# A decode-attention kernel whose TensorE program shrinks from 1307 to 449 instructions by loops over registers

## The chip, the core and the metric

The kernel runs on one core of one Trainium2 chip. A core has engines that run their own instruction streams and meet through semaphores: TensorE (PE, matrix products; loading of weights is shown as PEld), VectorE (DVE), ScalarE (ACT), GpSimd (POOL) and SyncE (SP), which here only issues DMAs. Sixteen DMA engines move data between the memory outside (DRAM) and the core's SBUF; PSUM takes the results of TensorE. The metric is the device time of one execution in microseconds (us); lower is better.

## What is computed

Two independent attention blocks, A and B, of one decode step each. `x` is one row of 512, there are 32 heads of 128, and the caches hold 8192 positions. Everything is bf16 in memory.

```python
q = (x @ wq).reshape(B, Sq, H, Dh).transpose(0, 2, 1, 3)       # 1 x 32 x 1 x 128
scores = einsum("bhqd,bhkd->bhqk", q, k_cache) * (Dh ** -0.5)  # 8192 per head
p = softmax(scores, axis=-1)
o = einsum("bhqk,bhkd->bhqd", p, v_cache)
y = o.transpose(0, 2, 1, 3).reshape(B, Sq, H * Dh) @ wo        # 512 per block
# output: concatenate([y of A, y of B], axis=-1)
```

The two pairs of caches hold 268 MB of the 285 MB that are read; each element is used once.

## The kernel before

The 64 heads form 16 groups of four (`N = 16`, groups 0 to 7 of A, 8 to 15 of B). A group is one round. Its K, 8 MiB, lies in SBUF with 32 partitions for a head and 256 positions (`T`) of 128 values in each partition; its V lies the same way. There are two buffers for K and one for V. At the start the V buffer holds the two wq, at the end the first K buffer holds the two wo.

**Start.** SP issues wq of A and B, K(0), K(1); V(0) waits until the q products have read wq. TensorE spreads x (L265) and multiplies it with wq (L282), ScalarE copies q into `qbc` (L288).

**A round n.** VectorE multiplies K in place with q, in two halves (`plan_mul`, L312). TensorE sums over d: for each of four tiles of 64 positions, 16 matmuls with the identity as weights and 512 columns of K as the moving operand add into one PSUM bank (`scores`, L468), and VectorE reduces the last eight columns (L317). Maximum (L324), its transposition (L487), the maximum of each head (L325), its spread (L490) give the bias of the exponential; ScalarE writes `pt` (four activations, L337), with zeros where a partition belongs to another head. TensorE sums the denominators (L496) and then runs PV: 256 matmuls with V as the weights and four columns of `pt` as the moving operand (L504). VectorE normalises (`plan_o`, L343 and L344).

**Order of DMAs.** All large loads are issued by SP in one order and run in that order: V(n) after PV(n-1) has read the buffer, K(n+2) after the scores of round n. For the last two rounds V comes in two parts, 192 positions and 64. After the scores of round 14, SP issues wo of A and 16 heads of wo of B; the rest of wo of B, in five DMAs of 8, 4, 2, 1 and 1 heads, stands behind V(15) (`WOB`, `load_wob`).

**Last round.** Between the maximum and PV of round 15 TensorE runs what is already possible of the output: four relayouts of finished heads (L392), the product of A with its wo (L407), 64 small matmuls for 16 heads of B (L420), and the sum for A (L429). After PV(15) it does the other 16 heads (L420) as their wo land. Block B's sum is copied (L439), transposed (L440), copied (L442) and written out by SP; block A's is written by ScalarE's queue.

**Programs.** A plan (`_Plan`, `op`, `wait`) collects each engine's instructions with a count for each semaphore; a line of `_emit` (L53) issues them, so DMAs carry L209. Only TensorE's rounds are a loop, `Fori(0, N)`, with both K buffers written out under `If`/`Else` and counts to wait for in registers (`_Stepped`). VectorE, ScalarE and SP have all 16 rounds written out.

Of the kernel before, what the change touches and what calls it, by code (L numbers as in the profile page):

```python
# [6 lines left out]
ALU = mybir.AluOpType  # L7
# [7 lines left out]
class _Ctr:  # L15


    def __init__(self, nc, stack, name):
        self.sem = stack.enter_context(nc.semaphore(name))
        self.n = 0  # L20
        self.name = name


class _Plan:


    def __init__(self):
        self.prog = {"SP": [], "PE": [], "ACT": [], "DVE": [], "POOL": []}
        self.waited = {}

    def wait(self, eng, mark):
        if mark is None:
            return
        ctr, val = mark
        if val <= 0 or self.waited.get((eng, ctr.name), 0) >= val:
            return
        self.waited[(eng, ctr.name)] = val
        self.prog[eng].append((None, ctr, val))

    def op(self, eng, fn, ctr=None, needs=(), inc=1):  # L40
        for m in needs:
            self.wait(eng, m)
        self.prog[eng].append((fn, ctr, inc))
        if ctr is None:
            return None
        ctr.n += inc
        return ctr, ctr.n


def _emit(e, items):  # L50
    for fn, ctr, k in items:
        if fn is None:
            e.wait_ge(ctr.sem, k)  # L53
        elif ctr is None:
            fn(e)
        else:
            fn(e).then_inc(ctr.sem, k)


class _Stepped:  # L60


    def __init__(self, e, ctr, first, step):
        assert first > 0 and step > 0
        self.e, self.ctr, self.step = e, ctr, step
        self.reg = e.alloc_register("w_" + ctr.name)
        e.reg_mov(self.reg, first)

    def wait(self):
        self.e.wait_ge(self.ctr.sem, self.reg)  # L70

    def grow(self):
        self.e.reg_add(self.reg, self.reg, self.step)


def bass_concat_heads__mha_block_cached__gqa_block_cached__decode_kernel(
# [35 lines left out]
    NM = 2  # L112
    HM = T // NM
    VT = 192


    WOB = [(0, 16, True), (16, 8, True), (24, 4, True), (28, 2, False), (30, 1, False), (31, 1, False)]
    NPRE = 1
    RG = [32, 16, 8, 4]
    NQ = NOUT // P  # L120

    with ExitStack() as st:
# [6 lines left out]
        kn = [sb("k%d" % i, [P, T, Dh], BF16) for i in range(2)]  # L129
        vn = sb("vn", [P, T, Dh], BF16)  # L130
        vflat = vn[:].rearrange("p t d -> p (t d)")
        kflat = [k[:].rearrange("p t d -> p (t d)") for k in kn]
        WQ = C * H * Dh
        wq_buf = [vflat[:, a * WQ:(a + 1) * WQ] for a in range(NA)]
        wq_sb = [b.rearrange("p (c n) -> p c n", c=C) for b in wq_buf]
        wo_buf = [kflat[0][:, a * H * NOUT:(a + 1) * H * NOUT] for a in range(NA)]
        wo_sb = [b.rearrange("p (j n) -> p j n", n=NOUT) for b in wo_buf]

        qmem = sb("qmem", [P, N * Dh // 2], F32)
        qbc = qmem[:].bitcast(BF16).rearrange("p (n d) -> p n d", d=Dh)  # L140
        ya_sb = qmem[:, 0:NOUT]
        pt = sb("pt", [P, T, G], BF16)
        s_sb = sb("s_sb", [P, T], F32)
        xrow = sb("xrow", [1, NA, D], BF16)
        xb = sb("xb", [P, NA, C, HP], BF16)
        ones_bf = sb("ones_bf", [P, P], BF16)
        ones_f = sb("ones_f", [P, P], F32)
        part = sb("part", [P, 1], F32)
        ident = sb("ident", [P, P], BF16)
        ident_f = sb("ident_f", [P, P], F32)  # L150
        m1 = sb("m1", [P, 1], F32)
# [4 lines left out]
        oD = sb("oD", [P, NA, H], BF16)  # L156
        zb = sb("zb", [P, 2, P], BF16)
        o2 = sb("o2", [P, NA, H], BF16)
        mask = {g: sb("mask%d" % g, [P, P // g], BF16) for g in RG}
        jsel = {g: sb("jsel%d" % g, [P, g], BF16) for g in RG}  # L160
        yT = sb("yT", [P, NQ], BF16)
        out_a = sb("out_a", [1, NOUT], BF16)
        out_b = sb("out_b", [NQ, P], BF16)

# [8 lines left out]
        yps = [ps("yps%d" % i, [P, 512]) for i in range(2)]  # L173

        pl = _Plan()
        op, wait = pl.op, pl.wait

        def ctr(name):
            return _Ctr(nc, st, name)

        s_x = ctr("s_x")
        s_w = [ctr("s_w%d" % a) for a in range(NA)]
        s_woa = ctr("s_woa")
        s_wob = [ctr("s_wob%d" % g) for g in range(len(WOB))]
        s_k = [ctr("s_k%d" % i) for i in range(2)]
        s_v, s_v2 = ctr("s_v"), ctr("s_v2")
        s_out = [ctr("s_out%d" % a) for a in range(NA)]
        c_pool, c_dve, c_act, c_pe = ctr("c_pool"), ctr("c_dve"), ctr("c_act"), ctr("c_pe")
        c_mul, c_sr, c_g, c_o, c_p = ctr("c_mul"), ctr("c_sr"), ctr("c_g"), ctr("c_o"), ctr("c_p")
        c_red, c_sum, c_pv, c_gx, c_bc = ctr("c_red"), ctr("c_sum"), ctr("c_pv"), ctr("c_gx"), ctr("c_bc")  # L190


        def red_done(n, h):
            return c_red, NB * n + h + 1

        def sum_done(n):
            return c_sum, n + 1

        def pv_done(n):
            return c_pv, n + 1  # L200

        def gx_done(n):
            return c_gx, n + 1

        def bc_done(n):
            return c_bc, n + 1

        def dma(eng, dst, src, c, needs=()):
            return op(eng, lambda e: e.dma_start(dst, src), c, needs, inc=16)  # L209


        def const(fn, needs=()):
            return op("POOL", fn, c_pool, needs)

        i_onesb = const(lambda e: e.memset(ones_bf[:], 1.0))
        i_onesf = const(lambda e: e.memset(ones_f[:], 1.0))
        const(lambda e: e.memset(part[:], 1.0 / HP))
        i_ident = const(lambda e: e.affine_select(
            out=ident[:], in_=ones_bf[:], pattern=[[1, P]], compare_op=ALU.is_equal,
            fill=0.0, base=0, channel_multiplier=-1), [i_onesb])  # L220
        i_identf = const(lambda e: e.affine_select(
            out=ident_f[:], in_=ones_f[:], pattern=[[1, P]], compare_op=ALU.is_equal,
            fill=0.0, base=0, channel_multiplier=-1), [i_onesf])
        const(lambda e: e.memset(rsum[:], 0.0))
        i_pool = const(lambda e: e.memset(pt[:], 0.0))


        x_in = [dma("ACT", xrow[0:1, a, :], xs[a][0], s_x) for a in range(NA)][-1]
        wq_in = [dma("SP", wq_buf[a], wqs[a].rearrange("(p c) n -> p (c n)", p=P), s_w[a])
                 for a in range(NA)]  # L230
        k_in, v_in = {}, {}

        def load_k(n):
            a, i = divmod(n, GA)
            src = ks[a][0, G * i:G * (i + 1)].rearrange("h (p t) d -> (h p) (t d)", p=HP)
            k_in[n] = dma("SP", kflat[n % 2], src, s_k[n % 2],
                          [red_done(n - 2, NB - 1) if n >= 2 else None])

        def load_v(n, need, t0=0, t1=T, c=None):
            a, i = divmod(n, GA)  # L240
            src = vs[a][0, G * i:G * (i + 1)].rearrange("h (p t) d -> (h p) (t d)", p=HP)
            v_in[n] = dma("SP", vflat[:, t0 * Dh:t1 * Dh], src[:, t0 * Dh:t1 * Dh], c or s_v, [need])

        wob_in = []

        def load_wob(g, need=None):
            h0, n, rows = WOB[g]
            src = wos[1][h0 * Dh:(h0 + n) * Dh, :]
            if rows:
                src = src.rearrange("(p j) n -> p (j n)", p=P)  # L250
                dst = wo_sb[1][:, h0:h0 + n, :].rearrange("p j n -> p (j n)")
            elif n == 1:
                dst = wo_sb[1][:, h0, :]
            else:
                src = src.rearrange("(j p) n -> p j n", p=P)
                dst = wo_sb[1][:, h0:h0 + n, :]
            wob_in.append(dma("SP", dst, src, s_wob[g], [need]))


        def xmm(e):  # L260
            r = None
            for a in range(NA):
                for c in range(C):
                    k = (a * C + c) * HP
                    r = e.matmul(misc[:, k:k + HP], xrow[0:1, a, c:D:C], ones_bf[0:1, 0:HP],  # L265
                                 start=True, stop=True)
            return r
        m = op("PE", xmm, c_pe, [x_in, i_pool])
        x_ready = op("ACT", lambda e: e.copy(
            xb[:].rearrange("p a c m -> p (a c m)"), misc[:, 0:NA * C * HP]), c_act, [m])  # L270
        y_free = [x_ready, x_ready]
        qbc_ready = {}
        q_done = None
        for a in range(NA):
            for j in range(GA // 4):
                def qmm(e, a=a, j=j):
                    r = None
                    for hh in range(G):
                        for c in range(C):
                            w = wq_sb[a][:, c, 16 * j * Dh:16 * (j + 1) * Dh].rearrange(  # L280
                                "p (i h d) -> p i h d", h=G, d=Dh)[:, :, hh, :]
                            r = e.matmul(  # L282
# [7 lines left out]
                for n in range(n0, n0 + 4):  # L290
                    qbc_ready[n] = y_free[j % 2]
# [256 lines left out]
```

## Time and profile before

| | |
|---|---|
| median of 3 runs | 667.93 us (667.76 to 668.25) |
| the profiled execution, its own time | 667.87 us |
| its span, first to last instruction | 665.9 us |
| mean granted TensorE clock | 0.71 |
| data read from memory | 285.21 MB, 428 GB/s over the span |

A view called the page gives busy time by engine and the DMA queues (packets, MB, share of 16 engines' span). The chain of waits follows back from the last instruction what released it; a row is start, duration, what, and "issue" is waiting for nothing that the profile shows. Rows of the timeline are start, duration, engine, line, operation, tiles, shapes, count and the idle time before. Windows give each engine's busy time in a stretch, the granted clock, the DMA share and GB/s.

### The profile page before, as it was taken

Reading aid. Unit: us, or ns where it says so; the run is one execution under the profiler, and the core shown is the slowest. Engines: PE = TensorE matmul, PEld = TensorE weight load, DVE = VectorE, ACT = ScalarE, POOL = GpSimd, SP = SyncE. Lnnn points to the kernel's source line nnn. Section 1 sums busy time; section 2 is a strip of 40 time slices with the busy share of each in tenths; the row PEclk is TensorE's granted clock in tenths of the full one; section 3 lists DMA queues with packets and bytes.
Section 4 is the critical chain, followed back from the end, with each engine's and each line's share of the span. In section 5 each row is a group of like instructions: output and inputs, shape, how many; then the busy total and the mean of one; then the engine's idle time right before and its main releaser. Section 6 shows DMA issues by size and latency. Waiting matters only on the chain.

```text
span 665.9 us, 11616 instructions
## 1 busy us (share of the span) xinstructions
PE 408.6 (61%) x5455; PEld 240.3 (36%) x5455; DVE 340.4 (51%) x182; ACT 62.7 (9%) x151; POOL 2.0 (0%) x11
## 2 busy tenths in 40 slices
PE   2209176774919476491947649293864929386788
PEld 1003153534315152431515343151534325152536
DVE  1046924748192654819165471917447291744720
ACT  1100202010020202002020200202020020202020
POOL 1000000000000000000000000000000000000000
PEclk9758658595866759596675959567595957759595
DMA  9999999999999999999999999999999999999996
GB/s 378 441 441 438 438 435 437 405 433 441 429 437 437 441 441 433 406 441 441 425 437 441 437 437 413 433 441 433 433 437 441 437 433 409 441 441 426 413 451 286
DMA packets 6341, 285.32 MB, mean 428 GB/s; under 512 B 699, under 2 KB 1214, under 8 KB 1342
## 3 DMA queue, kind: packets, MB, share of 16 engines
q1 hardware_dynamic: 6328, 285.22, 99.2%
q8 instruction: 5, 0.08, 0.0%
q14 instruction: 2, 0.02, 0.0%
q10 hardware_dynamic: 6, 0.00, 0.0%
HBM read 285.21 MB, written 0.00 MB: 428 GB/s over the span
## 4 chain that ended last, share of the span: by engine, by line
DMA 76%; PE 17%; DVE 3%; another core or an unknown queue 1%; issue 1%; ACT 1%; SPq 1%
DMA vn<-in_A_v_cache_dram 33%; DMA vn<-in_B_v_cache_dram 33%; PE acc L504 16%; DMA k<-in_A_k_cache_dram 6%; DMA k<-in_B_wo_dram 5%; DVE k L312 3%; PE rps L468 1%; ACT pt L337 1%; SPq L209 1%; DVE s_sb L317 0%; PE misc L496 0%; DVE m L324 0%; PE bmp L490 0%; PE mtp L487 0%
## 5 line engine op out<-in xcount | busy, mean ns | idle before, releaser
L312 DVE TENSOR_TENSOR k<-k,qmem 128x16384 bf16<-128x16384 bf16 x32 | 276.3, 8672 | 38.7 <-DMA k<-in_A_k_cache_dram 38.7
L468 PE MATMUL rps<-k,ident 128*128 128x512 bf16 x1024 | 258.6, 420 | 28.3 <-DVE k L312 24.5
L504 PE MATMUL acc<-pt,vn 128*128 128x4 bf16 x4096 | 111.9, 166 | 121.4 <-DMA vn<-in_A_v_cache_dram 63.3
L468 PEld LDWEIGHTS rps<-k,ident 128*128 128x128 bf16 x1024 | 107.4, 106 | 173.8 <-issue 75.8
L504 PEld LDWEIGHTS acc<-pt,vn 128*128 128x128 bf16 x4096 | 110.7, 104 | 122.7 <-DMA vn<-in_A_v_cache_dram 64.0
L317 DVE TENSOR_REDUCE s_sb<-rps 128x64 f32<-128x512 f32 x64 | 44.2, 691 | 213.1 <-PE rps L468 213.1
L330 ACT ACTIVATE negb<-bmp 128x4 f32<-128x4 f32 x16 | 2.8, 175 | 561.7 <-PE bmp L490 561.7
L337 ACT ACTIVATE pt<-s_sb,negb 32x256 bf16<-32x256 f32 x64 | 55.2, 862 | 1.9
L496 PE MATMUL misc<-rsum,ones_f 128*128 128x4 f32 x32 | 9.0, 351 | 59.0 <-ACT pt L337 59.0
L343 DVE RECIPROCAL rinv<-misc 128x4 f32<-128x4 f32 x16 | 2.9, 180 | 55.3 <-PE acc L504 55.3
L496 PEld LDWEIGHTS misc<-rsum,ones_f 128*128 128x128 f32 x32 | 8.0, 311 | 61.5 <-issue 61.5
L487 PE MATMUL mtp<-ident_f,m 128*1 128x128 f32 x32 | 6.1, 271 | 19.8 <-DVE m L324 19.8
L337 ACT ACTIVATION_READ_ACCUMULATOR pt<-s_sb,negb 32x1 f32 x64 | 15.9, 249 | 0.0
L282 PE MATMUL yps<-vn,xb 128*32 128x512 bf16 x64 | 7.2, 625 | 10.9 <-DMA vn<-in_B_wq_dram 6.1
L487 PEld LDWEIGHTS mtp<-ident_f,m 128*1 128x1 f32 x32 | 1.4, 81 | 27.7 <-DVE m L324 27.7
L490 PE MATMUL bmp<-gm,ones_f 1*128 1x4 f32 x32 | 6.1, 258 | 5.9 <-DVE gm L325 5.9
L490 PEld LDWEIGHTS bmp<-gm,ones_f 1*128 1x128 f32 x32 | 4.7, 182 | 10.6 <-DVE gm L325 10.6
L325 DVE TENSOR_REDUCE gm<-mtp 1x4 f32<-1x128 f32 x16 | 4.4, 278 | 7.5 <-PE mtp L487 7.5
L282 PEld LDWEIGHTS yps<-vn,xb 128*32 128x32 bf16 x64 | 2.7, 134 | 14.5 <-issue 7.6
L324 DVE TENSOR_REDUCE m<-s_sb 128x1 f32<-128x256 f32 x16 | 6.7, 420 | 0.5
L265 PE MATMUL misc<-ones_bf,xrow 1*128 1x32 bf16 x8 | 0.4, 190 | 8.0 <-DMA xrow<-in_B_x_dram 8.0
L288 ACT CAST qmem<-yps 128x512 bf16<-128x512 f32 x4 | 2.3, 587 | 16.0 <-PE yps L282 16.0
(38 smaller groups left out, 28.3 us busy)
## 6 DMA issues: line engine op xcount, KB each, us to landing
vn<-in_B_v_cache_dram SPq DMA_DIRECT2D x2, 6144.0 KB, 26.9
vn<-in_A_wq_dram SPq DMA_DIRECT2D x1, 4096.0 KB, 12.3
vn<-in_B_wq_dram SPq DMA_DIRECT2D x1, 4096.0 KB, 21.5
vn<-in_B_v_cache_dram SPq DMA_DIRECT2D x2, 2048.0 KB, 31.4
k<-in_A_wo_dram SPq DMA_DIRECT2D x1, 4096.0 KB, 25.1
k<-in_B_wo_dram SPq DMA_DIRECT2D x1, 2048.0 KB, 29.7
k<-in_B_wo_dram SPq DMA_DIRECT2D x1, 1024.0 KB, 33.5
k<-in_B_wo_dram SPq DMA_DIRECT2D x1, 512.0 KB, 34.3
```

The lines of the kernel that those rows point to most:

```text
L209: return op(eng, lambda e: e.dma_start(dst, src), c, needs, inc=16)
L282: r = e.matmul(yps[j % 2][hh * HP:(hh + 1) * HP, :].rearrange("p (i d) -> p i d", d=Dh), xb[:, a, c, :], w, start=(c == 0), stop=(c == C - 1))
L312: mul_done[n] = op("DVE", lambda e: e.tensor_tensor(k, k, qbc[:, n:n + 1, :].broadcast_to([P, HM, Dh]), ALU.mult), c_mul, [k_in[n], qbc_re ...
L317: sr_done[n, h] = op("DVE", lambda e: e.tensor_reduce(s_sb[:, h * HT:(h + 1) * HT], rps[:, h % 2, :].rearrange("p (t d) -> p t d", d=DW), ...
L324: op("DVE", lambda e: e.tensor_reduce(m1[:], s_sb[:], AX.X, ALU.max), c_g)
L325: op("DVE", lambda e: e.tensor_reduce(gm[:], mtp[0:1, 0:P].rearrange("o (h p) -> o h p", h=G), AX.X, ALU.max), c_g, [gx_done(n)])
L337: p_done[n] = op("ACT", lambda e, h=h, q=q: e.activation(pt[q, :, h], s_sb[q, :], AF.Exp, bias=negb[q, h:h + 1], scale=scale, accum_out=rs ...
L468: r = e.matmul(rps[:, h % 2, :].rearrange("p (t d) -> p t d", d=DW), ident[:], kn[slot][:, h * HT:(h + 1) * HT, i * DW:(i + 1) * DW], star ...
L487: e.matmul(mtp[0:1, 0:P], m1[:], ident_f[:], start=True, stop=True).then_inc(c_gx.sem, 1)
L490: e.matmul(bmp[:, 0:G], ones_f[0:1, :], gm[:], start=True, stop=True).then_inc(c_bc.sem, 1)
L496: e.matmul(misc[:, 0:G], ones_f[:], rsum[:], start=True, stop=True).then_inc(c_sum.sem, 1)
L504: m = e.matmul(acc[:, 0:G], vn[:, t, :], pt[:, t, :], start=(t == 0), stop=(t == T - 1))
```

## The change

The data, their tiles, the order of SP's loads and the arithmetic of softmax stay. What changes:

- **TensorE, scores.** One body for both K buffers; the place in K is a register (`koff`). A tile is cleared by a matmul of one row and one column, then a loop of four turns issues four matmuls each. VectorE is told at each turn (`c_red`) and waits for four.
- **TensorE, PV.** V is the moving operand: 64 matmuls of 512 columns (four positions) with 32 columns of `pt` as weights, into four strips of 32 PSUM partitions in turn. VectorE then masks the strips' useful parts (`prod`), adds them up (`om`), a matmul with `selh` gives the group's total (`total_of_group`), and VectorE normalises it (`outs`).
- **q.** x is transposed by four matmuls; 16 groups of four matmuls with all 128 output rows, in a loop; ScalarE copies four pieces of each.
- **Output.** A and 16 heads of B in 48 matmuls of 512 columns, in four strips; then copies and two fp32 matmuls add the strips; the last 16 heads of B in 32 matmuls of 256 columns. VectorE and ScalarE copy half each and SP writes the output in one DMA.
- **Loops.** VectorE's and ScalarE's rounds are loops. The programs of TensorE, VectorE and ScalarE stand inside a loop of one turn whose closing branch carries a hint (`once`).

```diff
+        def once(e):
+            one = e.alloc_register("once")
+            e.reg_mov(one, 1)
+            return nc.Fori(0, e.snap(one), engines=[e.engine], hint_back_edge=True)
...
-            def scores(slot, hs):
-                for h in hs:
-                    if h % (NB // NM) == 0:
-                        w_mul.wait()
-                        w_mul.grow()
-                    w_sr.wait()
-                    r = None
-                    for i in range(Dh // DW):
-                        r = e.matmul(
-                            rps[:, h % 2, :].rearrange("p (t d) -> p t d", d=DW), ident[:],
-                            kn[slot][:, h * HT:(h + 1) * HT, i * DW:(i + 1) * DW],
-                            start=(i == 0), stop=(i == Dh // DW - 1))
-                    r.then_inc(c_red.sem, 1)
-                    w_sr.grow()
+                def scores(tile):
+                    e.wait_ge(c_mul, by_tile)
+                    e.wait_ge(c_sr, by_tile)
+                    e.reg_add(by_tile, by_tile, 1)
+                    ro = rps[:, tile, :].rearrange("p (t d) -> p t d", d=DW)
+                    e.matmul(rps[:, tile, 0:1], zrow[:], ones_bf[0:1, 0:1], start=True, stop=False,
+                             skip_group_check=True)
+                    with e.Fori(0, NJ):
+                        k = e.snap(koff, min_val=0, max_val=2 * KS - HT * Dh + Dh - NI * DW)
+                        for i in range(NI):
+                            src = bass.AP(kn, k + i * DW, [[2 * KS, P], [Dh, HT], [1, DW]])
+                            m = e.matmul(ro, ident[:], src, start=False, stop=False, skip_group_check=True)
+                        m.then_inc(c_red, 1)
+                        e.reg_add(koff, koff, NI * DW)
...
+                def total_of_group():
+                    e.wait_ge(c_st, by_round)
+                    e.matmul(mtp[:, EX:EX + G], om[:], selh[:], start=True, stop=True).then_inc(c_ex, 1)
...
+                with e.Fori(0, N) as r:
+                    with e.Fori(0, NB // 2):
+                        for tile in range(2):
+                            scores(tile)
+                            e.reg_add(koff, koff, HT * Dh - Dh)
+                    e.reg_alu(koff, koff, 2 * KS - 1, op=ALU.bitwise_and)
...
+                    with e.If(r > 0):
+                        total_of_group()
+                    with e.If(r == N - 1):
+                        mid()
...
-                for t in range(T):
-                    if t == VT:
-                        with e.If(r >= N - 2):
-                            w_v2.wait()
-                            w_v2.grow()
-                    m = e.matmul(acc[:, 0:G], vn[:, t, :], pt[:, t, :],
-                                 start=(t == 0), stop=(t == T - 1))
-                m.then_inc(c_pv.sem, 1)
+                    for g in range(NG):
+                        if g * W == VT:
+                            with e.If(r >= N - 2):
+                                w_v2()
+                        k = g % G * HP
+                        m = e.matmul(acc[k:k + HP, :], ptf[:, g * W * G:g * W * G + HP],
+                                     vn[:, g * W * Dh:(g + 1) * W * Dh], start=(g < G), stop=(g >= NG - G))
+                    m.then_inc(c_pv, 1)
...
+                for g in range(1, len(WOB)):
+                    h0, n, rows = WOB[g]
+                    if g == 2:
+                        total_of_group()
+                    e.wait_ge(s_wob[g], 16)
+                    if not rows:
+                        e.wait_ge(c_o, N + 1)
+                    for h in range(h0, h0 + n):
+                        for b in range(2):
+                            m = e.matmul(yps[1][b * HP:b * HP + NA, 0:NH], o2[:, H + h, :],
+                                         wo_rows(H + h)[:, b * NH:(b + 1) * NH], start=False,
+                                         stop=(h == H - 1), skip_group_check=True)
+                m.then_inc(c_y, 1)
...
+                def part():
+                    w_pv()
+                    e.tensor_tensor(prod[:], acc[:].rearrange("p (t d) -> p t d", d=Dh),
+                                    msk[:].unsqueeze(2).broadcast_to([P, W, Dh]), ALU.mult).then_inc(c_self, 1)
+                    w_self()
+                    e.tensor_reduce(om[:], prod[:].rearrange("p t d -> p d t"), AX.X,
+                                    ALU.add).then_inc(c_st, 16)
+                    w_o()
+                    e.reciprocal(rinv[:], misc[:, 0:G]).then_inc(c_self, 1)
...
+                with e.Fori(0, N) as r:
+                    with e.If(r % 2 == 0):
+                        muls(0, r * Dh)
+                    with e.Else():
+                        muls(1, r * Dh)
+                    with e.If(r > 0):
+                        part()
...
+            e.wait_ge(c_yd, 2)
+            e.wait_ge(c_ya, 1)
+            e.dma_start(out[0].rearrange("o (a n) -> (o a) n", a=NA), out_sb[:]).then_inc(s_out, 16)
+            e.wait_ge(s_out, 16)
```

More of the change, by code (lines that the diff above doesn't have):

```diff
@@ L188, in bass_concat_heads__mha_block_cached__gqa_block_cached__decode_kernel @@
[L188 to L230, printed above, removed]
@@ L260, in xmm @@
-        def xmm(e):
-            r = None
-            for a in range(NA):
[L263 to L270, printed above, removed]
@@ L341, in plan_o @@
[L341 to L356 removed]
+        EX = 128
@@ L427, in bass_concat_heads__mha_block_cached__gqa_block_cached__decode_kernel @@
-        for g in range(NPRE):
-            mm_b(g)
-        m = op("PE", lambda e: e.matmul(mtp[0:1, :], part[:], ya_sb, start=True, stop=True),
-               c_pe, [ya_ready, misc_free[0]])
-        m = op("ACT", lambda e: e.copy(out_a[:], mtp[0:1, :]), c_act, [m])
-        done_a = dma("ACT", out[0][:, 0:NOUT], out_a[:], s_out[0], [m])
-        mid1 = len(pl.prog["PE"])
-        plan_o(N - 1)
-        for g in range(NPRE, len(WOB)):
-            m = mm_b(g)
-        m = op("DVE", lambda e: e.tensor_copy(yT[:], yps[1][:, 0:NQ]), c_dve, [m])
```

562 lines of the change are left out of this document (279 added, 283 removed).

## The prediction

> **What bounds the kernel now.** I read the page first (engines, DMA queues), then the chain of waits, then the windows between the landings it names.
>
> ```profile
> span 665.9 us, 11616 instructions
> ...
> PE 408.6 (61%) x5455; PEld 240.3 (36%) x5455; DVE 340.4 (51%) x182; ACT 62.7 (9%) x151; POOL 2.0 (0%) x11
> ...
> q1 hardware_dynamic: 6328, 285.22, 99.2%
> q8 instruction: 5, 0.08, 0.0%
> q14 instruction: 2, 0.02, 0.0%
> ```
>
> No engine is near its limit; the data queue is, at 99.2% of 16 DMA engines. The two instruction queues carry almost nothing, but look where that little falls. The chain of waits in order of time:
>
> ```profile
> 1.73 40.43 DMA k<-in_A_k_cache_dram
> ...
> 74.07 8.04 another core or an unknown queue
> ...
> 86.45 3.22 issue
> ...
> 92.56 28.26 DMA vn<-in_A_v_cache_dram
> ...
> 127.88 31.64 DMA vn<-in_A_v_cache_dram
> ...
> 553.59 31.64 DMA vn<-in_B_v_cache_dram
> ...
> 592.29 26.82 DMA vn<-in_B_v_cache_dram
> ...
> 628.96 34.17 DMA k<-in_B_wo_dram
> ...
> 663.17 0.28 PE yps L420 x4
> ...
> 664.00 0.28 DVE out_b L442
> ```
>
> K(0) lands at 42.16, V(0) at 82.11 (74.07 + 8.04), V(1) at 120.82, V(2) at 159.52, and so on to V(13) at 585.23: from V(1) on, 12 steps in (585.23 - 120.82), 38.70 us each for two transfers of 8 MiB, so 19.35 us each. But K(0) to V(0), also two such transfers, took 39.95. The 1.25 us lost there is never made up. The windows between these landings (last two columns: mean DMA share, GB/s):
>
> ```profile
> 42.16:82.11 39.95, 16.97 (x70) 7.35 (x70) 33.54 (x10) 3.63 (x9) 0.00 (x0) 0.71 0.97 421
> 82.11:120.81 38.70, 25.18 (x326) 14.73 (x326) 17.32 (x11) 3.63 (x9) 0.00 (x0) 0.68 1.01 434
> ```
>
> The instruction queues in the list of DMA queues: the first row is that of each of these two stretches, the second that of 120.81 to 660, where q8 has none:
>
> ```profile
> q8 instruction: 2, 0.03, 0.3%
> ...
> q14 instruction: 2, 0.02, 0.0%
> ```
>
> 0.97 x 39.95 = 38.75: the mean DMA engine needed its usual time; the transfer was complete 1.25 us late. So a few engines were late, not all. The stretch holds the first two instruction fetches (0.08 MB in 5, 16 KB each); two more follow in the next, then none of TensorE's. My reading: a fetch goes to one DMA engine, takes about 1.25 us of it, and that engine, never idle, stays late to the end, where the last landing waits for it. That later fetches add nothing says that each falls on another engine. The end agrees:
>
> ```profile
> 658.00:660.00 2.00, 2.00 (x81) 2.00 (x79) 0.00 (x0) 0.00 (x0) 0.00 (x0) 0.50 0.97 392
> 660.00:662.00 2.00, 1.73 (x60) 1.58 (x58) 0.34 (x2) 0.00 (x0) 0.00 (x0) 0.50 0.82 280
> 662.00:664.00 2.00, 1.50 (x33) 1.09 (x31) 0.17 (x2) 0.00 (x0) 0.00 (x0) 0.50 0.09 33
> ```
>
> Work left at 660 is (0.82 + 0.09) x 2 = 1.82 us of every engine; evenly spread it would end at 661.82, not 663.12.
>
> **The change part by part.**
>
> *Fetches.* TensorE's 1307 instructions become 449, VectorE and ScalarE loop, and closing branches carry hints. 1307 over five fetches is some 260 a fetch, so 449 are under two such blocks; before, no fetch is seen until scores(0), so I take two blocks to be there at the start. If no fetch is left while data flows, the last landing moves from 663.12 to 661.87: -1.25. The other bound is 0: one fetch left makes one engine late again. I take -1.25, as nothing in the new program needs a third block. [...]
>
> *After the last landing.* Before: 663.12 to the output's DMA, 1.18 (628.96 + 34.17 above, the last row below). Now: 0.05, two matmuls of 256 columns (as the 0.28 of L420), 0.04, one copy of 2x256, halves on VectorE and ScalarE at once, 0.04. The copy lies between 0.28 (L442, 4x128) and 0.58 (L431, 1x512); I take 0.40. Sum 0.81: -0.37 (bounds -0.49, -0.19). Prices, from the timeline:
>
> ```profile
> 22.85 3.64 PE L282 MATMUL yps<-vn,xb 128*32 128x512 bf16 x32 [6.08 <-DMA vn<-in_B_wq_dram]
> ...
> 60.13 7.08 PE L468 MATMUL rps<-k,ident 128*128 128x512 bf16 x32 [0.55 <-DVE s_sb L317]
> ...
> 626.42 16.20 PE L468 MATMUL rps<-k,ident 128*128 128x512 bf16 x64 [0.27 <-issue]
> ...
> 642.65 0.69 DVE L317 TENSOR_REDUCE s_sb<-rps 128x64 f32<-128x512 f32 x1 [2.76 <-PE rps L468]
> ...
> 644.60 0.38 PE L490 MATMUL bmp<-gm,ones_f 1*128 1x4 f32 x2 [0.37 <-DVE gm L325]
> ...
> 646.99 2.67 PE L407 MATMUL yps<-k,o 128*32 128x512 bf16 x32
> ...
> 651.39 1.87 PE L429 MATMUL mtp<-qmem,part 128*1 128x512 f32 x2
> ...
> 653.18 0.59 PE L496 MATMUL misc<-rsum,ones_f 128*128 128x4 f32 x2
> ...
> 653.29 0.58 ACT L431 CAST out_a<-mtp 1x512 bf16<-1x512 f32 x1 [4.51 <-PE mtp L429]
> ...
> 653.63 6.97 PE L504 MATMUL acc<-pt,vn 128*128 128x4 bf16 x256
> ...
> 664.30 0.35 SPq L209 DMA_DIRECT2D out_dram<-out_b  x1
> ```
>
> *PV* (256 pairs in 6.97) becomes 64 matmuls of 512 columns in four column strips. Such matmuls ran 32 in 3.64 at clock 0.5 and 32 in 2.67, so 64 take 5.3 to 7.3; I take 6.0.
>
> *Scores.* 64 matmuls at 7.08/32 = 0.221 are 14.2 at the full clock; before, the first ones ran at the low clock after PV's four-column matmuls (16.20 in all). Added: four clearing matmuls (half of L490's 0.38 each, 0.8) and 16 loop turns with address arithmetic and a branch. The trace has no such turn. The nearest row is the idle time before a round's first score, where a closing branch and register additions also lie:
>
> ```profile
> PE rps L468 <- issue: 2.4, 9, 0.4
> PE acc L504 <- DMA vn<-in_A_v_cache_dram: 63.3, 8, 9.1
> PE acc L504 <- DMA vn<-in_B_v_cache_dram: 54.9, 7, 9.1
> ```
>
> So 0 to 0.4 a turn; I take 0.1, since four matmuls (0.88) run meanwhile and the sequencer can work ahead. Scores: 14.2 + 0.8 + 1.6 = 16.6, against 16.20.
>
> *Rounds 0 to 14* hide all this: TensorE waits for V 118.2 us in 15 times, 7.9 each, and the queue hides more:
>
> ```profile
> vn<-in_A_wq_dram SPq DMA_DIRECT2D x1, 4096.0 KB, 12.3
> ...
> 26.57 0.33 SPq L209 DMA_DIRECT2D vn<-in_A_v_cache_dram  x1
> ...
> 144.25 0.33 SPq L209 DMA_DIRECT2D k<-in_A_k_cache_dram  x1
> ```
>
> V(2), issued at 127.88 (chain), follows a K that has the engines until 120.82 + 19.35 = 140.2: 12 us spare; K at 144.25 follows V(2), done at 159.5: 15 spare. V(0) now waits for 16 q groups. A group is four matmuls at twice 0.221 (1.8, low clock) plus ScalarE's copies and waits, say 2.2: 35 us from the landing of the first wq (12.3 in flight, so 13): 48 instead of 26.57, and K(1) keeps the engines until 42.16 + 19.35 = 61.5. Scores(0), 6 us later than at present, still send K(2) out well before V(0) is done. Nothing is lost; were the spare time gone, a later issue would add itself to every round. VectorE's new product and reduction (0.69 each as L317) stand ahead of the score reductions, but these wait for TensorE, and VectorE is 51% busy.
>
> *The last round* has no cover; TensorE must keep up with the landing. PV(14) starts when its V lands (592.29 + 26.82) less 1.25, at 617.9, and ends at 623.9 (before 626.15). Scores(15) end at 640.7 (before 642.6). Maximum and negative bias, 2.4 as before: 643.1. Then, new and in TensorE's order ahead of the rest, the group total that waits for VectorE's reduction (long done), 0.59 as L496, and its product: 643.9. Four relayouts, 2.0 as between L490's end and L407 before: 645.9. 48 Wo matmuls at 2.67/32 to 3.64/32, 4.0 to 5.5, say 4.7: 650.6. Copy 0.69: 651.4. Two fp32 matmuls of 256 columns, between half and all of L429's 1.87, say 1.4, and L496: 653.4. PV(15): 659.4 (before 660.6). Product and reduction, 1.5: 660.9. Group total, 0.59: 661.5; normalisation 0.2: 661.7. Eight matmuls for the last four heads, 0.6: 662.3. By the landing it would be 661.87 + 0.05 + 0.28 = 662.2. The two meet; I add 0.1.
>
> **Sum**: -1.25 - 0.37 + 0.1 = -1.5 on the profiled execution's 667.87 (the span and 1.97 around it), so 666.4; the median of the runs is 667.93, the same within 0.1.
>
> **Rivals.** (1) *A fetch stays.* One is enough for one late engine. For: the profile shows two small fetches of q14, and I see no row of a hinted branch. Then only the tail gains, 667.5; a turn of 0.15 to 0.25 us lands in the same place, 667.2 to 668.8.
>
> (2) *Loop turns on TensorE cost what a round's closing costs* (slower). Place: the score loop in round 15, where 16 turns stand on the path to PV(15). Each 0.1 us more is 1.6 us. From 0.28 a turn the time passes 669.3; at 0.4 it is 666.4 + 16 x 0.3 = 671.2; I price it at 670. Against: the 0.4 is the longest of nine.
>
> (3) *Taken branches refetch code.* The row 86.45 is one such stall, 3.22 us, in the first pass through PV. If every closing branch caused it, rounds 0 to 14 would hide it (7.9 each), round 15 would not, and 16 fetches more would make some engines late two or three times, 2.5 to 3.8: 666.4 + 3.2 + 2, about 671. Against: before, the loop also closes 15 times, and 3.22 comes once. [...]
>
> **How the numbers follow.** Forecast 666.4, own range 665.8 to 666.6: 0.47. Rival 1 with the middling turns: 0.23. Rival 2: 0.24. Rival 3: 0.06. Within 0.2% (1.3 us) a measurement of this kernel can hardly tell a change, so faster means under 666.6, slower over 669.3: faster 0.47, same 0.23, slower 0.30. The range runs from 665.8 (both terms at their best, -1.30 and -0.49, with the rest of the fetch queues' delay) to 671.0, leaving out rival 3 and the worst of rival 2, some 0.15.
>
> **What would show it.** Right: no instruction fetch between the first and last data packet; K(0) to V(0) in 38.7; last Wo landing near 661.9; scores(15) near 16.6; TensorE waiting for that landing. Wrong: a q8 packet in the run, a landing still at 663, or scores over 19 us with TensorE busy through to the output.

## The result, and the profile after

The changed kernel takes 667.08 us (median of 20 runs, 665.97 to 667.98) against 668.00 for the kernel before (20 runs, 667.76 to 668.45): a ratio of 0.9984 with an interval of 0.9977 to 0.9991, 0.92 us faster. The interval leaves out 1, so the gain is real, but it is under the 0.2% from which the prediction speaks of a change: by its classes this is "same". The forecast was 666.4. The profiled execution took 667.75, 0.12 less than the one of before.

The page of the changed kernel, engines and DMA queues:

```profile
span 665.7 us, 7894 instructions
...
PE 384.7 (58%) x2397; PEld 170.0 (26%) x2397; DVE 368.4 (55%) x217; ACT 76.0 (11%) x211; POOL 2.3 (0%) x12
...
q1 hardware_dynamic: 6324, 285.22, 99.2%
q14 instruction: 1, 0.01, 0.0%
```

q8 is gone, and one q14 packet is left; it comes at the very end, after the data. K(0) lands at 42.31 and V(0) at 81.01; the window between them (last three columns: granted clock, DMA share, GB/s):

```profile
42.31:81.01 38.70, 18.87 (x74) 7.96 (x74) 29.42 (x10) 3.62 (x9) 0.00 (x0) 0.72 1.00 434
```

38.70 instead of 39.95: the loss of 1.25 us is not there. The windows at the end:

```profile
652.00:656.00 4.00, 2.77 (x48) 1.35 (x48) 0.00 (x0) 0.00 (x0) 0.00 (x0) 1.00 0.97 414
656.00:658.00 2.00, 0.95 (x16) 0.39 (x16) 0.00 (x0) 0.00 (x0) 0.00 (x0) 0.96 0.98 410
658.00:660.00 2.00, 0.74 (x10) 0.35 (x8) 1.64 (x3) 0.00 (x0) 0.00 (x0) 0.50 0.98 389
660.00:662.00 2.00, 2.00 (x20) 1.16 (x16) 0.20 (x3) 0.00 (x0) 0.00 (x0) 0.50 0.67 218
662.00:664.00 2.00, 1.66 (x16) 0.74 (x12) 0.43 (x2) 0.30 (x1) 0.00 (x0) 0.50 0.00 0
```

Before, 0.09 of the engines' time after 662 still went into data (0.09 x 2 us x 16 engines = 2.9 us, some engines late by about 1); now 0.00. The data end about 1 us earlier, but look at the clock: 0.50 from 658 on, with TensorE busy through to 663.66. The timeline of the same stretch says what it does there:

```profile
650.50 0.39 PE L469 MATMUL misc<-rsum,ones_f 128*128 128x4 f32 x2
652.15 2.77 PE L477 MATMUL acc<-vn,pt 128*32 128x512 bf16 x48 [1.27 <-DMA vn<-in_B_v_cache_dram]
657.05 1.16 PE L477 MATMUL acc<-vn,pt 128*32 128x512 bf16 x16 [2.13 <-DMA vn<-in_B_v_cache_dram]
...
659.47 1.87 PE L491 MATMUL yps<-kn,o 128*2 128x256 bf16 x16 [1.26 <-DMA kn<-in_B_wo_dram]
661.27 0.59 PE L426 MATMUL mtp<-selh,om 128*128 128x4 f32 x2
661.79 1.87 PE L491 MATMUL yps<-kn,o 128*2 128x256 bf16 x16
...
663.70 0.41 DVE L336 CAST out_sb<-yps 2x256 bf16<-2x256 f32 x1 [1.57 <-PE yps L491]
664.15 0.33 SPq L219 DMA_DIRECT2D out_dram<-out_sb  x1
```

The second group of 16 (L491) has no wait in front of it: TensorE is still behind when the last Wo has landed. The output's DMA starts at 664.15, against 664.30 before. So in this execution almost all of what the queue gained went into TensorE's last 4.2 us (659.47 to 663.66).

The spans of the 20 runs fall into two groups: 664.2 to 664.7 in 8 runs (665.97 to 666.88 us), 665.2 to 666.2 in 12 (666.93 to 667.98 us). The profiled run is one of the 12.

### The profile page after: what moved, and what is told of

Read it like the earlier page. It is cut to its first block, busy times and chain, and to the rows that moved or that the text cites. A ratio compares the mean times of both kernels' runs of the same rounds, so it can differ in the third digit from the quotient of the medians.

```text
span 665.7 us, 7894 instructions
## 1 busy us (share of the span) xinstructions
PE 384.7 (58%) x2397; PEld 170.0 (26%) x2397; DVE 368.4 (55%) x217; ACT 76.0 (11%) x211; POOL 2.3 (0%) x12
## 4 chain that ended last, share of the span: by engine, by line
DMA 82%; PE 16%; issue 1%; ACT 1%; ACTq 0%; SPq 0%; DVE 0%
DMA vn<-in_A_v_cache_dram 41%; DMA vn<-in_B_v_cache_dram 34%; PE acc L477 13%; DMA kn<-in_B_wo_dram 5%; PE yps L402 2%; DMA vn<-in_A_wq_dram 2%; ACT qmem L356 1%; PE yps L491 1%; SPq L191 0%; ACTq L356 0%; PE mtp L426 0%; ACTq L26 0%; DVE out_sb L336 0%
## 5 line engine op out<-in xcount | busy, mean ns | idle before, releaser
L265 DVE TENSOR_TENSOR kn<-kn,qmem 128x16384 bf16<-128x16384 bf16 x32 | 276.7, 8688 | 49.1 <-DMA kn<-in_A_k_cache_dram 37.0
L420 PE MATMUL rps<-kn,ident 128*128 x1024 | 236.6, 383 | 0.4
L477 PE MATMUL acc<-vn,pt 128*32 128x512 bf16 x1024 | 90.8, 532 | 155.4 <-DMA vn<-in_A_v_cache_dram 81.1
L420 PEld LDWEIGHTS rps<-kn,ident 128*128 128x128 bf16 x1024 | 96.5, 98 | 110.8 <-issue 22.6
L477 PEld LDWEIGHTS acc<-vn,pt 128*32 128x32 bf16 x1024 | 38.3, 128 | 201.2 <-issue 194.4
L270 DVE TENSOR_TENSOR prod<-acc,msk 128x512 f32<-128x512 f32 x16 | 11.0, 690 | 44.2 <-PE acc L477 44.2
L402 PE MATMUL yps<-vn,xT 128*128 x64 | 17.7, 429 | 10.2 <-DMA vn<-in_A_wq_dram 6.0
L414 PE MATMUL rps<-ones_bf,zrow 1*128 1x1 bf16 x64 | 11.0, 172 | 15.2 <-DVE kn L265 15.1
L356 ACT CAST qmem<-yps 32x128 f32 x64 | 16.4, 256 | 11.4 <-PE yps L402 10.7
L273 DVE TENSOR_REDUCE om<-prod 128x128 f32<-128x512 f32 x16 | 16.6, 1039 | 1.9
```

What stands on the lines that cost most here:

```text
L265: e.tensor_tensor(k, k, qflat[:, bass.ds(q, Dh)].unsqueeze(1).broadcast_to([P, HM, Dh]), ALU.mult).then_inc(c_mul, 2)
L270: e.tensor_tensor(prod[:], acc[:].rearrange("p (t d) -> p t d", d=Dh), msk[:].unsqueeze(2).broadcast_to([P, W, Dh]), ALU.mult).then_inc(c_ ...
L273: e.tensor_reduce(om[:], prod[:].rearrange("p t d -> p d t"), AX.X, ALU.add).then_inc(c_st, 16)
L356: i = e.copy(qflat[p, bass.ds(r * (2 * Dh) + j * Dh, Dh)], yps[j][p, h * Dh:(h + 1) * Dh])
L402: i = e.matmul(yps[j][:], xT[:, bass.ds(x0 + c, 1)].broadcast_to([P, P]), vn[:, bass.ds(w0 + (c * H * Dh + j * G * Dh), G * Dh)], start=(c ...
L414: e.matmul(rps[:, tile, 0:1], zrow[:], ones_bf[0:1, 0:1], start=True, stop=False, skip_group_check=True)
```

## Experiments

Two theories were to be tested. First, that an instruction fetch makes one DMA engine late and that this lateness lasts to the end. Second, that the tail of the changed kernel is set by the granted clock: TensorE waits 2.1 us for V and 1.3 us for Wo, its clock falls over these waits (1.00 at 652 to 656, 0.50 from 658 on), and its last work is done at 0.50. Each ratio is to the kernel before on the same chip (668.0 to 668.1 throughout), its 95% interval in brackets. A slot is one place in TensorE's program as it is built: 483 in the changed kernel, 1318 in the one before (the title's 449 and 1307 are another count).

### One fetch put back, by the hint or by more code

Without the hint:

```diff
-            return nc.Fori(0, e.snap(one), engines=[e.engine], hint_back_edge=True)
+            return nc.Fori(0, e.snap(one), engines=[e.engine], hint_back_edge=False)
```

> The closing branches of the one-turn loops carry no hint any more; all else as in the changed kernel. [...] Rival (the short program alone does it, hints do nothing): no instruction packet in the run, last landing 662.1, time as the changed kernel, 666.0 to 668.0 with a median near 667.1.

667.85 us (667.27 to 669.0), ratio 1.0002 [0.9993, 1.0011]: the gain is gone. The rival fails: one q8 packet is back in the run, between 74 and 76 us, and the time lies in the 667.4 to 668.4 that the author estimated for that case:

```profile
q8 instruction: 1, 0.02, 0.0%
...
662.00:664.00 2.00, 1.68 (x24) 0.91 (x20) 0.44 (x2) 0.27 (x1) 0.00 (x0) 1.00 0.03 11
```

(the page's queue, then the window at the end). Data flow again after 662. The delay can be followed from the fetch to the end. The chain's row of V(0) in the changed kernel, then the rows of V(0) and of the first Wo products after PV(15) without the hint:

```profile
36.17 44.84 DMA vn<-in_A_v_cache_dram
```

```profile
35.18 47.05 DMA vn<-in_A_v_cache_dram
...
660.71 1.64 PE L491 MATMUL yps<-kn,o 128*2 128x256 bf16 x16 [0.70 <-DMA kn<-in_B_wo_dram]
```

V(0) lands at 82.23 instead of 81.01, and 580 us later the first Wo is still 1.2 us late (660.71 against 659.47). The packet itself occupies one engine for about 1.06 us (3.3% of 16 engines' 2 us; in the kernel before, the one at 54 to 56 takes 3.2%, 1.02 us). The profiled span is nevertheless the changed kernel's 665.7, because here TensorE's clock is back at 1.00 after 662. The 11 spans fall into two groups again, 665.3 to 665.8 and 666.8 to 667.0, with medians 1.2 and 1.35 above those of the changed kernel's groups.

With the hint left in, code was added ahead of round 0, once with 130 extra matmuls of one column, once with 260, into a column of PSUM that nothing reads:

```diff
                 e.wait_ge(c_sel, 11)
+                for _ in range(130):
+                    e.matmul(bmp[:, 8:9], zrow[:], ones_bf[0:1, 0:1], start=True, stop=True)
```

> 130 added matmuls of one column, run once on TensorE before round 0 while it waits for K(0): some 260 more instructions, so a third block of code. Theory (a fetch makes one DMA engine late by 1.0 to 1.3 us to the end): at least one packet of 16 KB on q8 in the run, the last Wo lands at 662.9 to 663.4, time 667.4 to 668.4. Rival (fetches cost nothing, the 1.25 us of before came from TensorE's own stall): packet or not, last landing 662.1 and the time unchanged, median near 667.1.

> 260 added matmuls of one column instead of 130, some 520 more instructions, so two more blocks. Theory (each fetch falls on another engine, and one late engine is enough): one packet of 16 KB more than with 130, the last landing the same as there, 662.9 to 663.4, within 0.2 of it. Rival (the delays add up on one engine): 664.0 to 664.6. Rival (fetches cost nothing): 662.1.

130: 670.30 us (669.22 to 671.87), ratio 1.0034 [1.0022, 1.0046]. 260: 671.63 (670.79 to 672.32), ratio 1.0052 [1.0039, 1.0066]. The last windows, the first kernel's and then the second's:

```profile
660.00:662.00 2.00, 1.49 (x16) 0.84 (x16) 1.11 (x2) 0.00 (x0) 0.00 (x0) 0.50 0.69 228
662.00:664.00 2.00, 2.00 (x18) 1.24 (x16) 0.17 (x1) 0.00 (x0) 0.00 (x0) 0.50 0.02 7
```

```profile
660.00:662.00 2.00, 1.25 (x14) 0.76 (x16) 1.24 (x3) 0.00 (x0) 0.00 (x0) 0.57 0.70 233
662.00:664.00 2.00, 2.00 (x18) 1.22 (x16) 0.16 (x1) 0.00 (x0) 0.00 (x0) 0.50 0.05 19
```

After 662 the one has 0.02 x 2 x 16 = 0.6 us of engine time left, the other 0.05 x 32 = 1.6: read as one late engine and two. The first kernel has one packet in the run (at 40 us), the second two (at 40 and 48). Their lateness doesn't add up: the first Wo products begin at 660.51 and 660.75, the spans are 666.7 and 667.0. So the first Wo products come 1.0 and 1.3 us later than in the changed kernel (659.47), with one packet as with two, and 1.2 us later without the hint, where the packet comes at 75 instead of 40. What was not expected: the times rose by 3.2 and 4.6 us over the changed kernel's, more than the spans. In both profiled runs a further q8 packet comes after the output, outside the span, and the time around the span is 3.6 and 4.6 us, against 2.0 in the changed kernel's.

### TensorE kept busy in the waits of the tail

Extra matmuls, whose results nothing reads, fill the two waits: seven ahead of V's second part in the last round, five ahead of the last Wo products.

```diff
+                def busy(n):
+                    for _ in range(n):
+                        e.matmul(rps[:, 0, :], ident[:], vn[:, 0:512], start=True, stop=True)
...
                         if g * W == VT:
+                            with e.If(r == N - 1):
+                                busy(7)
                             with e.If(r >= N - 2):
                                 w_v2()
...
+                busy(5)
                 for g in range(1, len(WOB)):
```

> In round 15 TensorE fills two waits with matmuls whose result nobody reads: 7 of 512 columns before the second part of V(15), 5 after PV(15). Theory (after the last landing TensorE's low clock sets the end: 1.87 us for 16 matmuls that take 0.95 at the full clock): granted clock 1.00 from 652 to the end, the output's DMA issued near 662.8 instead of 664.15, time 666.0 to 666.6 in nearly every run, with less spread than the changed kernel's 665.97 to 667.98. Rival (the order of the tail, the wait for the group's total, sets the end whatever the clock): time 667.0 to 668.0 and the same spread.

667.53 us (667.24 to 667.87), ratio 0.9992 [0.9983, 1.0001]. The clock did what the theory says, the time didn't. Page and windows:

```profile
q8 instruction: 1, 0.02, 0.0%
...
658.00:660.00 2.00, 1.93 (x21) 0.80 (x21) 0.73 (x2) 0.00 (x0) 0.00 (x0) 1.00 0.95 382
660.00:662.00 2.00, 1.83 (x26) 1.10 (x26) 1.15 (x3) 0.00 (x0) 0.00 (x0) 1.00 0.76 251
662.00:664.00 2.00, 1.22 (x16) 0.33 (x10) 0.51 (x2) 0.36 (x1) 0.00 (x0) 1.00 0.02 6
```

Clock 1.00 to the end, spread 0.63 instead of 2.0; but the 27 slots more that this straight-line program takes brought a q8 packet (between 74 and 76 us), and 0.02 after 662 is one late engine again. The same matmuls in a loop take 14 slots, 497 in all:

```diff
-                    for _ in range(n):
+                    with e.Fori(0, n):
```

(and without an `If` of its own: `busy(7)` stands inside `e.If(r >= N - 2)`, so it runs in the last two rounds).

> [...] Theory (the changed kernel's tail is set by TensorE at the low granted clock, and the straight-line run lost its gain to a third code block): no packet on the instruction queues, 16 engines ending within 0.5 us, last Wo landing at 662.1, granted clock 1.00 to the end, the output's DMA at 662.9 instead of 664.15, time 666.2 (665.8 to 666.6) with a spread under 0.7. Rival A (497 slots are already too many): one packet of the instruction queue at 75, one engine at 663.1, time 667.5 as in the straight-line run. Rival B (the clock in the tail doesn't matter, the end is the queue's): time stays 667.1.

669.70 us (667.54 to 670.11), ratio 1.0020 [1.0011, 1.0030], slower than the kernel before, although the span came out as expected, 664.5, with no fetch in it. The timeline's end, and the DMA queues from 663 on, past the span's end:

```profile
660.77 0.60 PE L497 MATMUL yps<-kn,o 128*2 128x256 bf16 x8
661.53 0.95 PE L497 MATMUL yps<-kn,o 128*2 128x256 bf16 x8 [0.16 <-DMA kn<-in_B_wo_dram]
662.52 0.36 ACT L370 CAST out_sb<-yps 2x256 bf16<-2x256 f32 x1 [14.67 <-PE yps L497]
...
662.97 0.33 SPq L219 DMA_DIRECT2D out_dram<-out_sb  x1
```

```profile
q8 instruction: 1, 0.02, 0.4%
q14 instruction: 1, 0.01, 0.2%
```

TensorE now waits for the landing (0.16 us in the second row), as the prediction had it, its clock is 1.00 in every window from 652 to 664, and the output goes out 1.18 us earlier than in the changed kernel (662.97 against 664.15). But a q8 packet comes after the output, and the time around the span is 5.0 to 5.4 us in ten of eleven runs instead of 1.7 to 2.6. Neither rival as written holds: the fetch is there, but not at 75.

### The same with a smaller program, a control, and one wait alone

The Q projection's loop was made to run over 16 groups instead of 8 pairs, which takes 11 slots off:

```diff
-        yps = [ps("yps%d" % i, [P, 512]) for i in range(2)]
+        y2 = ps("y2", [P, 1024])
+        yps = [y2[:, i * 512:(i + 1) * 512] for i in range(2)]
...
-                with e.Fori(0, N // 2) as r:
...
+                with e.Fori(0, N) as r:
...
-                    for j in range(2):
...
-                            i = e.matmul(
-                                yps[j][:], xT[:, bass.ds(x0 + c, 1)].broadcast_to([P, P]),
...
+                    y0 = (r % 2) * 512
...
+                        i = e.matmul(
+                            y2[:, bass.ds(y0, 512)], xT[:, bass.ds(x0 + c, 1)].broadcast_to([P, P]),
```

once with the looped extra matmuls (486 slots), once without (472). A third kernel is the changed one with the first set of extra matmuls alone, without `busy(5)` (490 slots; the changed kernel has 483).

> The looped extra matmuls of the tail, as in the run before last that had them, with the program made smaller elsewhere: the Q projection's loop goes over 16 groups instead of 8 pairs (both accumulators in one tensor, chosen by a register), 11 slots fewer, 486 in all against 497. Theory (what the larger program lost is the third code block, fetched after the output at the end; the tail itself is won by the clock): no instruction packet of TensorE anywhere, the span 664.4 as there, the time 1.7 to 2.1 over the span instead of 5.3: 666.3 (666.0 to 666.6), spread under 0.8, and faster than both kernels. Rival A (the 3 us outside the span come from the extra matmuls themselves, not from the size): time 669.5 again. Rival B (486 is still too many): 3 us outside, or a fetch early in the run and a landing at 663.

> Control: the smaller Q loop alone, 472 slots, no extra matmuls. Theory: the changed kernel's time of 667.1 with its two groups of runs (spans near 664.4 and near 665.5), since nothing of the tail is touched; the Q projection lies in the cover of K(1). Rival (the spread of the changed kernel comes from the code blocks, 483 slots being near the limit): spread under 0.8 and a median near 666.3.

> The changed kernel with the first set of looped extra matmuls only (those ahead of the wait for the second part of V), 490 slots. Where the block ends: 485 slots ran without a third block, 497 with one; if 490 are within, the time is 1.7 to 2.6 over the span, if not, 3.3 to 5.3. The clock: if the wait for V is what cools TensorE, the clock stays at 1.00 to the end and spans are 664.4; if the wait after PV(15) does it, the Wo matmuls run at 0.5 as in the changed kernel and spans lie at 665.3 to 666.

486 slots with both sets: **666.06 us** (665.94 to 666.48, 7 runs), ratio 0.9971 [0.9959, 0.9982], the best of all. Spans 664.2 to 664.7, 1.73 to 1.79 around them. Its windows:

```profile
656.00:658.00 2.00, 1.10 (x17) 0.59 (x19) 0.00 (x1) 0.00 (x0) 0.00 (x0) 1.00 0.99 414
658.00:660.00 2.00, 2.00 (x19) 0.84 (x19) 1.81 (x3) 0.00 (x0) 0.00 (x0) 1.00 0.98 387
660.00:662.00 2.00, 1.85 (x26) 0.80 (x20) 0.17 (x1) 0.00 (x0) 0.00 (x0) 1.00 0.66 211
662.00:664.00 2.00, 0.27 (x2) 0.08 (x2) 0.41 (x1) 0.36 (x1) 0.00 (x0) 1.00 0.02 5
```

The control: 666.53 us (666.07 to 667.77, 8 runs), ratio 0.9981 [0.9971, 0.9992]. It has the two groups again, five spans at 664.3 to 664.5 and three at 665.4 to 665.7, so the smaller program alone doesn't end the spread (five short runs of eight against eight of twenty are too few to say that it changes the shares). Its profiled run is one of the five, and shows what the shorter group is:

```profile
656.00:658.00 2.00, 1.09 (x12) 0.53 (x16) 0.00 (x0) 0.00 (x0) 0.00 (x0) 0.72 1.00 418
658.00:660.00 2.00, 1.48 (x16) 0.43 (x10) 1.04 (x2) 0.00 (x0) 0.00 (x0) 0.50 0.96 381
660.00:662.00 2.00, 2.00 (x29) 1.12 (x26) 0.93 (x3) 0.00 (x0) 0.00 (x0) 0.92 0.65 209
```

Here too the clock falls, but earlier, and it is back at 0.92 between 660 and 662, in time for the last products; in the changed kernel's profile it fell later and stayed at 0.50. That the moment at which the clock falls and returns makes the two groups is argued from these two profiles; no kernel has a profile of both groups. What is shown is that matmuls in the waits hold the clock at 1.00 and that the longer group is then gone: spans of 664.2 to 664.8 in all 7 runs here and in all 11 of the looped matmuls above, 1.00 in every window from 652 on in both profiles.

The first set alone: spans 664.2 to 664.5 in all 11 runs and a clock of 1.00 in every window from 652 to 664, with 1.36 us of waiting for Wo left as it was, so the wait for V is the one that matters. But the time is 669.42 us (666.38 to 670.1), ratio 1.0014 [1.0005, 1.0023]: 490 slots are too many in ten runs of eleven (4.3 to 5.6 around the span); the eleventh, with 2.0, is the 666.38.

### What a turn of TensorE's loop costs

```diff
-    NI = 4
+    NI = 2
```

and `NI = 1`: the same matmuls in 32 or 64 turns a round; then two matmuls a turn with the looped extra matmuls (485 slots).

> Two matmuls instead of four in each turn of the score loop: 32 turns a round instead of 16, the same matmuls, 12 slots fewer. Theory (a turn is worked ahead by the sequencer while matmuls run, and costs nothing as long as the matmuls of a turn last longer than its bookkeeping): scores of round 15 stay at 15.3 to 15.8 us, time 666.9 to 667.5. Rival (a turn costs 0.1 us on the path, the value that the prediction took): scores 16.9, time 667.1 to 668.7, since the wait for the second part of V (2.1 us) can take up some of it. At 0.28 a turn: scores 19.8, time over 669.

> One matmul in each turn of the score loop: 64 turns a round. Theory (the bookkeeping of a turn is hidden by its matmuls as long as these last longer): a turn has 0.22 us of matmul, so the scores of round 15 show the cost of a turn wherever that is over 0.22: at 0.10 they stay near 15.5 and the time near 667.1; at 0.30 they are 20 us and the time is about 667.1 + 4.7 - 2.1 = 669.7. Rival (0.1 a turn always lies on the path): scores 15.35 + 4.8 = 20.2 too, but then the run with 32 turns shows 16.9.

> Two matmuls a turn (32 turns a round) together with the looped extra matmuls of the tail: 485 slots, two more than the changed kernel. If turns cost nothing and the low clock is what the changed kernel lost: no instruction packet, landing 662.1, time 666.2 as the looped extra matmuls alone, and that even where 497 slots should prove too many. If turns cost 0.1: the wait for the second part of V takes up 1.6 us of its 2.1, so the time is still under 666.6, while the scores show 16.9.

Two a turn: 668.99 us (667.49 to 669.64), ratio 1.0011 [1.0002, 1.0020]. One a turn: 806.70 us, ratio 1.2071 [1.2055, 1.2088]. Two with extra matmuls: 671.57 us, ratio 1.0059 [1.0045, 1.0073], where 666.2 to 666.6 had been expected. A tile of scores in round 15 on the timelines of four matmuls a turn, of two, and (from an earlier round) of one:

```profile
624.54 3.63 PE L420 MATMUL rps<-kn,ident 128*128 x16
628.10 0.17 PE L414 MATMUL rps<-ones_bf,zrow 1*128 1x1 bf16 x1
...
636.05 3.73 PE L420 MATMUL rps<-kn,ident 128*128 x16
641.19 0.38 PE L461 MATMUL mtp<-ident_f,m 128*1 128x128 f32 x2 [1.41 <-DVE m L297]
```

```profile
635.00 5.10 PE L420 MATMUL rps<-kn,ident 128*128 x16
640.16 0.16 PE L414 MATMUL rps<-ones_bf,zrow 1*128 1x1 bf16 x1
640.38 5.08 PE L420 MATMUL rps<-kn,ident 128*128 x16
```

```profile
581.09 1.86 PE L420 MATMUL rps<-kn,ident 128*128 x4
583.11 1.86 PE L420 MATMUL rps<-kn,ident 128*128 x4 [0.15 <-issue]
```

One a turn: four turns in 583.11 - 581.09 = 2.02 us, 0.50 each, while the matmul needs 0.22. Two: 5.10 / 8 = 0.64 a turn, matmuls 0.44. Four: 3.63 / 4 = 0.91, matmuls 0.88. A turn costs the sequencer about 0.37 and each matmul 0.13 more (0.64 - 0.50), which for four is 0.89: an estimate from the two shorter loops, and level with the matmuls. So turns cost next to nothing at four matmuls and show in full below; both theories as sized were wrong (scores of round 15 with two a turn took 645.46 - 624.20 = 21.3 us, not 15.5 or 16.9). With one a turn TensorE becomes the bound of every round: in the groups of instructions PV waited 155.4 us for V in the changed kernel (first row), and 0.0 here.

```profile
L477 PE MATMUL acc<-vn,pt 128*32 128x512 bf16 x1024 | 90.8, 532 | 155.4 <-DMA vn<-in_A_v_cache_dram 81.1 <-DMA vn<-in_B_v_cache_dram 74.3
...
L477 PE MATMUL acc<-vn,pt 128*32 128x512 bf16 x1024 | 86.3, 511 | 0.0
```

The third kernel, with 485 slots, has 1.7 us around its span and no q8 packet: it puts the limit above 485. Its miss of 5 us lies in the span (669.4 in the profiled run). With scores of 21 us TensorE is late for V(15), so the waits that the extra matmuls were to fill are not there, and they stand on the path: 1.55 us ahead of the second part of PV(15), 1.3 after it, and the output goes out at 667.81, against 664.57 with two a turn alone.

Two things here do not fit a count of slots. The kernel with one matmul a turn has the smallest program, 465 slots, and yet a q8 packet at 803.5, just behind its output, with only 1.7 us around the span of that run. And with two a turn, 471 slots, seven of eleven runs have 2.5 to 2.9 us around the span; the profiled one, with 1.9 and no q8 packet, does not say why.

## Why the prediction was right, and where it wasn't

**The number.** 667.08 lies in the wide range, but above the own range of 665.8 to 666.6, and the class with the highest chance, a time under 666.6, did not come. "Same" did, for another reason than the one that its 0.23 was given for: no fetch stayed.

**Fetches: right.** -1.25 was forecast for the last landing, to 661.87; the stretch from K(0) to V(0) became shorter by exactly that, K(0) itself came 0.15 later (42.31 against 42.16), and no data move after 662. Rival 1 (a fetch stays) is what the kernel without the hint shows: the hint is needed (no q8 packet with it, one without), and one late engine is enough. How the hint does that, and which code the packet brings, is not shown. Two steps towards it were weak. The time of 1.25 us that one engine was to lose to a fetch measures 1.0 to 1.06 a packet, and V(0) comes 1.0 to 1.3 us late in the four kernels that fetch ahead of it. And the two blocks there at the start were an assumption that no run shows; the 260 instructions a fetch don't agree with it, since five fetches and two blocks would make seven for 1307. That no q8 packet came was partly luck: the prediction did not know how near the limit was.

**After the last landing: right in size, not in what sets it.** The copy takes 0.41 (0.40 assumed). But the output waits for TensorE, not for the landing.

**The last round up to PV(15): too dear by 2.5 us.** Scores(15) ended at 639.8 (forecast 640.7), since a tile takes 3.63 and a turn next to nothing; TensorE was ready for PV(15) at 650.89 (650.50 + 0.39; forecast 653.4). It bought nothing, because the prediction had left out that V(15) must land: TensorE waited 1.27 us for its first part, until 652.15, and 2.13 us for its second.

**The step that failed** is the last of that sum, "Eight matmuls for the last four heads, 0.6: 662.3", and with it "the two meet". The mechanism, that TensorE must keep up with the landing, was right, the term was mis-sized. After PV(15) 16 heads are left, two matmuls each. I gave no time to the first 12 and priced the last four at nearly the full clock. But the Wo of the first 8 lands only just before 659.47 (the wait in front of that row), and then their 16 matmuls, the group's total and 16 more for the other 8 heads follow at a clock of 0.50: 1.87, 0.59 and 1.87, ending at 663.66 instead of 662.3. At a clock of 1.00 the same 32 take 1.04 and about 1.55, the total 0.38, and TensorE waits for the landing (the looped extra matmuls). The prediction had no wait of TensorE in the last round, and so no fall of the clock; filling the wait for V's second part alone holds it at 1.00 from 652 to 664. 8 of the 20 runs have about the forecast's time (665.97 to 666.88), the other 12 move the median 0.7 above it. In the 8 the clock is probably back in time, as in the profile of the control; none of them was profiled. The clock falls at different moments: in 656 to 658 its mean is 0.96 in the changed kernel's profile and 0.72 in the control's. What sets the moment is not shown.

**Rival 2 (turns at 0.4): the price was right, the cover held.** A turn does cost the sequencer some 0.4 us and 0.13 more for each matmul, by the estimate above, but beside four matmuls of 0.88 us it stays hidden. The forecast's 0.1 a turn for the path was too much (0.91 against 0.88), and the margin to the rival was nearly nil: that four matmuls a turn are just enough was luck.

**Rival 3 (refetch at taken branches): wrong.** No q8 packet appears in any of 16 rounds of the changed kernel. (The stall of 3.22 us at 86.45 in the kernel before does hold one, at 86 to 88.) What the runs show is how narrow that is: 486 slots fit, 490 mostly don't. What sets this limit is not shown.

## What to carry to other kernels

Where a balanced stream of data fills the time, as here, reckon with what instruction fetches of 16 KB cost at its end in these runs, 1.0 to 1.3 us, once, with one as with two; keep the program so small that none falls into the run, count slots before adding even a dozen instructions, and look past the span's end for a late block. Where TensorE waits and then has to finish behind the last transfer, price its work at the low clock (0.50 here), or keep it busy in the wait, if there is one. Compare a loop's turn on TensorE with its matmuls: here four matmuls a turn were nearly free (0.91 us for 0.88 of matmuls), two (0.64 for 0.44) and one (0.50 for 0.22) were not.

## What the runs showed that was not expected

Kernels with a q8 packet after the output mostly lost more here than those with one during the run. With 27 slots more than the changed kernel the block came at 75 us: 667.53 in all, about 2.0 around the span. With 14 more it came after the end: 669.70, 5.3 around the span, though the span was 0.8 shorter (664.5 against 665.3); with 7 more the profile shows the same, a q8 packet at 666 to 667 and 5.0 around the span. That this packet is what takes the 3 us is argued, not shown: the kernel with one matmul a turn had one behind its output without the loss. A profile whose span falls while the time rises is to be read at the queues behind the span.
